# Block 6 wholly in half products, a norm of twelve operations, and other orders at the ends of blocks 1, 2 and 5

## The chip, the cores and the metric

The kernel runs on one core of a Trainium2 chip. The metric is device time in microseconds (us). The engines are named as in the profile: PE is TensorE (matrix products), PEld its weight loads, DVE is VectorE, ACT is ScalarE, POOL is GpSimd, and SP issues transfers.

## What is computed

The reference is a linear attention without softmax, a norm over each head, and a gated GELU layer on its result:

```python
# q, k, v: (8, 8, 576, 64)
kv  = np.einsum('bhsd,bhse->bhde', k, v)
out = np.einsum('bhsd,bhde->bhse', q, kv)
rms = np.sqrt(np.mean(out * out, axis=-1, keepdims=True) + 1e-06)
a   = out / rms * g_norm
x   = a.transpose(0, 2, 1, 3).reshape(4608, 512)     # tokens x channels
# w_gate, w_val: (512, 1536); w_out: (1536, 512); w_res: (512, 512)
g, val   = x @ w_gate, x @ w_val
ffn_out  = (gelu(g) * val) @ w_out
out      = x + sigmoid(x @ w_res) * ffn_out          # (4608, 512)
```

## The kernel before

The 4608 tokens are taken in nine blocks of 512. Blocks 0 to 7 hold 512 of the 576 tokens of batches 0 to 7. Block 8 holds the 64 that are left of each. While block m runs through the gated layer, the attention of batch m+2 is computed beside it, and its result t (FP16) is written as soon as its norm is there.

A block has twelve slices f of the 1536 hidden columns, for the gate (g) and for the value (v). A slice can be done plainly, four products of 128x512 for each of g and v. Or four slices are done as a group in **half products**: seven products of half matrices (256 token columns) in place of eight, after Strassen and Winograd. They need sums of the weights (`ws`), formed once, and sums of the tokens (`ts`), formed once in each block. `GROUPS` says which of the three groups of a block are in half products:

```python
GROUPS = {blk: (1, 2) for blk in range(2, B - 1)} | {B - 1: (1, 0, 2), B: (0, 1, 2)}   # B = 8
```

So blocks 2 to 6 do group 0 plainly, as slices 0 to 3, and blocks 7 and 8 do all three groups in half products. Two helpers compute these pieces:

```python
def m_gval(blk, f, pool=pmoe, tag="mm"):          # one plain slice
    gps = pool.tile([P, NJ * P], FP32, ...);  m_mm(gps, wg_c, f, blk, 0, NJ)   # 4 matmuls 128x512
    vps = pool.tile([P, NJ * P], FP32, ...);  m_mm(vps, wv_c, f, blk, 0, NJ)   # 4 matmuls 128x512
    m_act(blk, f, gps, vps)                       # ACT: ge = gelu(gps);  DVE: hid = ge * vps
# gv_group: a half-product group. A digit is a product (4 matmuls 128x256), E and d are copies
# on ACT, F and c are sums on DVE, g11.. a GELU on ACT, h11.. a product on DVE (h22 on POOL).
for word in """1g 1v Eg 5g Ev 5v dg 6g dv 6v Fg 2g Fv 2v 7g g11 7v cg 3g cv 3v h11 g22 4g
               g12 h12 4v g21 h22 h21""".split():
    ...
    for f in amid.get(word, ()):                  # work of other stages that is placed behind a word
        f()
```

After its groups a block has the products with `w_res` (`rps`) and then the seven half products of the output layer. Between these stand the sums, the gate (`pf`), and the sum with x (`fin`, on POOL). At the places named `aside` other stages put work of theirs:

```python
def others():                                     # second part of a block's output layer
    prod(w["A"], s_[1], wo_t[:, 1], False)
    aside("F");  sub(nc.vector, w["F"], w["A"], w["d"], ALU.add)
    aside("00"); prod(w["E"], ...); pf((0, 0), w["E"])
    aside("22"); prod(w["A"], s_[2], ...)
    c22 = res_all[part((1, 1))]
    sub(nc.vector, c22, w["A"], w["d"], ALU.add)  # reads bank A before it is written again
    aside("01"); prod(w["F"], ...); pf((0, 1), w["F"])
    if not later: fin((0, 0))
    aside("11"); prod(w["A"], ...); pf((1, 1), c22); pf((1, 0), w["A"])
    if later: return                              # block 1: its fins are in block 2
    fin((0, 1)); store(0); fin((1, 1)); fin((1, 0)); store(1)
if later:
    at_word(blk + 1, 0, "h21", *x[0:2], fin((0, 0)), fin((0, 1)), store(0))
    at_word(blk + 1, 1, "Fv", x[2])
    at_word(blk + 1, 1, "h21", x[3], fin((1, 0)), fin((1, 1)), store(1))
# the four sums ts of a block's tokens, on DVE, in the output layer of the block ahead
for blk in GROUPS:
    for key, f in zip(("00", "22", "01", "11"), token_sums(blk, nc.vector)):
        aside_out(blk - 1, key, f)
```

The norm of batch b takes 1/sqrt of a 128x40 tile by an integer guess and three Newton steps. From batch 2 on it runs on POOL with fifteen operations. The scalings `a_t` (t = o times that, on DVE, out of the four PSUM banks of o) follow it:

```python
tensor_scalar(m  = ss / D + eps); tensor_scalar(yy = guess(m)); tensor_scalar(mh = -0.5 * m)
for _ in range(3):
    tensor_tensor(a = yy * yy); tensor_tensor(a = a * mh)
    tensor_scalar(a = a + 1.5); tensor_tensor(yy = a * yy)          # on POOL
...
aside_out(m, "F", lambda: a_norm(b, 0, NJ + rem, pool))             # m = b - 2
at(m, NF + 3, lambda: new_block(b), lambda: a_t(b, 0), lambda: a_t(b, 1))   # behind others()
for j in range(2, NJ + rem):
    at(m + 1, j - 2, lambda j=j: a_t(b, j))                         # behind plain slices 0, 1, 2
```

POOL also issues the loads of q, k and v of the next batch (`load_behind`, behind group 1 of the block). It is in order[...].

Of the kernel before, what the change touches and what calls it, by code (L numbers as in the profile page):

```python
# [8 lines left out]
FP32 = mybir.dt.float32  # L9
# [9 lines left out]
def kernel(  # L19
# [15 lines left out]
    nc = tc.nc  # L35
# [59 lines left out]

    def load_qr(b):
        if b % 2 == 0:
            qr_t[b // 2] = qkvp.tile([P, C], FP16, tag="qr", name="qr")
# [182 lines left out]
        nc.scalar.copy(out=st[b]["kv2"], in_=st[b]["ps"][0])  # L281

    def rem_out(b):
        st[b]["o"][NJ] = o32 = attnp.tile([P, C], FP32, tag="o32", name="o32")
        for e in range(2):
            nc.scalar.copy(
                out=o32.rearrange("p (r e d) -> p r e d", e=2, d=D)[:, :, e, :], in_=st[b]["ps"][1][e]
            )

    def a_norm(b, j0, j1, eng=nc.vector):  # L290

        s = st[b]
        if "rinv" not in s:
            s["rinv"] = attnp.tile([P, NJ + 1, H], FP32, tag="ny", name="ny")
        ss, yy = (t[:, j0:j1, :].rearrange("p j h -> p (j h)") for t in (s["ss"], s["rinv"]))
        n = (j1 - j0) * H
        m = attnp.tile([P, (NJ + 1) * H], FP32, tag="nm", name="nm")[:, 0:n]
        a = attnp.tile([P, (NJ + 1) * H], FP32, tag="na", name="na")[:, 0:n]
        mh = attnp.tile([P, (NJ + 1) * H], FP32, tag="nh", name="nh")[:, 0:n]
        eng.tensor_scalar(out=m, in0=ss, scalar1=1.0 / D, scalar2=RMS_EPS, op0=ALU.mult, op1=ALU.add)  # L300
        eng.tensor_scalar(
            out=yy.bitcast(I32), in0=m.bitcast(I32), scalar1=-0.5, scalar2=float(0x5F3759DF), op0=ALU.mult, op1=ALU.add
        )
        eng.tensor_scalar(out=mh, in0=m, scalar1=-0.5, scalar2=None, op0=ALU.mult)
        for _ in range(3):
            eng.tensor_tensor(out=a, in0=yy, in1=yy, op=ALU.mult)
            eng.tensor_tensor(out=a, in0=a, in1=mh, op=ALU.mult)
            if eng is nc.vector:
                eng.scalar_tensor_tensor(out=yy, in0=a, scalar=1.5, in1=yy, op0=ALU.add, op1=ALU.mult)
            else:  # L310
                eng.tensor_scalar(out=a, in0=a, scalar1=1.5, scalar2=None, op0=ALU.add)
                eng.tensor_tensor(out=yy, in0=a, in1=yy, op=ALU.mult)  # L312

    def pair(b):

# [38 lines left out]
        )  # L354

    def d_rem_qT(b):
        st[b]["qrT"] = attnp.tile([P, NP, P], FP16, tag="qrT", name="qrT")
        nc.sync.dma_start(out=st[b]["qrT"], in_=qr_t[pair(b)], transpose=True)

    def d_xT(b, j0, j1):  # L360
# [127 lines left out]
    def out_by_products(blk, later, banks, amid):  # L488
        w = {}
        s_ = hid_sums  # L490

        def aside(ahead_of):
            for f in amid.get(ahead_of, ()):
                f()

        def res(jj):
            for j in (2 * jj, 2 * jj + 1):
                m_res(blk, j, banks[j])

        def first_two():  # L500
            for n in ("D", "E", "F", "A"):
                w[n] = pmoe.tile([P, 2, CH], FP32, name="w" + n, bank=banks[n])
            w["d"] = finp.tile([P, 2, CH], FP32, tag="wd", bufs=1, name="wd")
            s_last(blk)
            prod(w["A"], a_of(blk, 1, 1), b_of(1, 1), True)
            nc.scalar.copy(out=w["E"], in_=w["A"])
            aside("D")
            prod(w["D"], s_[0], wo_t[:, 0], True)
            nc.scalar.copy(out=w["d"], in_=w["D"])
            aside("gates")  # L510
            for j in range(NJ):
                m_sigmoid(j)

        def part(jj):
            return slice(None), slice(2 * jj[0], 2 * jj[0] + 2), slice(jj[1] * CH, (jj[1] + 1) * CH)

        def pf(jj, src):
            nc.vector.tensor_tensor(out=res_all[part(jj)], in0=th_all[part(jj)], in1=src, op=ALU.mult)  # L518

        def fin(jj):  # L520
            of = part(jj)
            nc.gpsimd.tensor_tensor(out=res_all[of], in0=res_all[of], in1=t_t[blk][of], op=ALU.add)  # L522

        def store(jj):
            dst = out[blk * S : blk * S + M0, :].rearrange("(p j) c -> p j c", j=NJ)
            js = slice(2 * jj, 2 * jj + 2)
            nc.sync.dma_start(out=dst[:, js, :], in_=res_all[:, js, :])

        def others():


            prod(w["A"], s_[1], wo_t[:, 1], False)
            aside("F")
            sub(nc.vector, w["F"], w["A"], w["d"], ALU.add)
# [19 lines left out]
            fin((0, 1))  # L554
            store(0)
            fin((1, 1))
            fin((1, 0))
            store(1)

        if later:  # L560
            x = [lambda j=j: a_x(blk, j) for j in range(NJ)]
            at_word(blk + 1, 0, "h21", *x[0:2], lambda: fin((0, 0)), lambda: fin((0, 1)), lambda: store(0))
            at_word(blk + 1, 1, "Fv", x[2])
            at_word(blk + 1, 1, "h21", x[3], lambda: fin((1, 0)), lambda: fin((1, 1)), lambda: store(1))
        return [lambda: res(0), lambda: res(1), first_two, others]

    def out_last(blk, banks):
# [22 lines left out]
        def run():  # L590
            wa = [bank(1, banks["A"][e]) for e in range(2)]
            wd, we, wf = [bank(2, banks[n]) for n in "DEF"]
            d = finp.tile([P, 2, CH], FP32, tag="wd", bufs=1, name="wd")
# [58 lines left out]
    def weight_sums(unit, eng):  # L652
# [3 lines left out]

        def one(s_, x, y, op):
            if s_ == 0:
                pool, tag = (wpool, f"ws{n}{g}") if g > 0 else (qkvp, "k16")
                gv_sums[unit] = pool.tile([P, 4, 2, 2, P], FP16, tag=tag, name="ws")  # L660
# [189 lines left out]
    for n, t in (("g", moe_w_gate), ("v", moe_w_val)):  # L850
# [4 lines left out]
    ident32 = consts.tile([P, P], FP32, name="ident32")  # L855
    make_identity(nc, ident32)

    zeros = consts.tile([P, C], FP16, name="zeros")
    nc.vector.memset(zeros, 0.0)
    mask = consts.tile([P, P], FP32, name="mask")  # L860
# [15 lines left out]
    grow32 = consts.tile([1, 2, D], FP32, name="grow32")  # L876
    nc.vector.tensor_copy(out=grow32, in_=grow[:, None, :].to_broadcast([1, 2, D]))
    grow16 = consts.tile([1, H, D], FP16, name="grow16")
    nc.vector.tensor_copy(out=grow16, in_=grow[:, None, :].to_broadcast([1, H, D]))
    for t in last_kv[0] + last_kv[1]:  # L880
        nc.vector.memset(t[R:P], 0.0)
# [332 lines left out]
    def banks_of(blk):  # L1214
# [16 lines left out]
                groups[i].update({(u, "A"): a0, (u, "E"): e, (u, "F"): f})  # L1231
        (ga0, ge_, gf, ga1), (va0, ve, vf, va1) = g, v
        if blk not in LAST:
            out_at[blk] = {0: ge_, 1: ga1, 2: ve, 3: ge_, "A": va1, "D": ga1, "E": ve, "F": ge_}
            att_at[blk] = [gf, vf, ga0, va0]
            pmoe.turn = [out_at[blk][n] for n in "DEFA"]
# [128 lines left out]
```

## Time and profile before

| | us |
|---|---|
| time, median of three | 330.12 (329.43 to 330.67) |
| span of the profiled execution | 328.4 |
| PE busy | 317.6 |
| DVE busy | 261.3 |
| ACT busy | 193.3 |
| POOL busy | 143.5 |

Busy time is time with an instruction in work on that engine. The span less PE's busy time is the time in which PE had nothing in work. Where it stood idle, and for whom, is read from the list of waits and from the timelines of single engines.

### The profile page before, as it was taken

To read this page: it belongs to the slowest core of one execution; us is meant where nothing else is said; L and a number is where in the kernel's file an instruction comes from. 1 tells how busy PE (TensorE), PEld (TensorE's weight loads), DVE (VectorE), ACT (ScalarE), POOL (GpSimd) and SP (SyncE) were. 2 spreads that over 40 slices of the span, in tenths; PEclk is the share of its full clock that TensorE was granted. 3 is DMA by queue.
4 is the path that set the end of the run, shared out by engine and by line. 5 is a ranking of instruction groups with operands and counts; after the bars stand their busy time and mean duration, and the time that the engine had idled before them with its cause. 6 is when DMAs were issued, how large, how long until landed. Compare 5 with 4: busy or idle time off the path is not lost.

```text
span 328.4 us, 7217 instructions
## 1 busy us (share of the span) xinstructions
PE 317.6 (97%) x2840; PEld 227.1 (69%) x2840; DVE 261.3 (80%) x474; ACT 193.3 (59%) x351; POOL 143.5 (44%) x222
## 2 busy tenths in 40 slices
PE   8999999999989999899999999999999999999993
PEld 3545655445848785686768686868587888788882
DVE  5777879679598995988887888697889877687754
ACT  3764676465537782668376846674465466636660
POOL 2783333574701498428731974115511331051232
PEclk9999999999999999999999999999999999999998
DMA  8999999898985349577949693800340030011004
GB/s 251 322 204 204 195 204 161 181 189 122 180 85 109 100 98 187 157 140 92 135 147 143 73 153 130 162 1 3 128 82 0 8 123 1 2 64 66 0 3 128
DMA packets 76692, 38.87 MB, mean 118 GB/s; under 512 B 42098, under 2 KB 74354, under 8 KB 76658
## 3 DMA queue, kind: packets, MB, share of 16 engines
q0 software_dynamic: 38752, 17.17, 41.7%
q1 hardware_dynamic: 37328, 20.71, 24.4%
q10 hardware_dynamic: 578, 0.52, 0.5%
q8 instruction: 22, 0.36, 0.5%
q14 instruction: 12, 0.10, 0.1%
HBM read 38.80 MB, written 9.44 MB: 147 GB/s over the span
## 4 chain that ended last, share of the span: by engine, by line
PE 82%; DVE 6%; POOL 5%; DMA 3%; issue 2%; ACT 0%; DVEq 0%; POOLq 0%; ACTq 0%
PE Av L723 9%; PE Ag L723 9%; PE gps L386 9%; PE wA L479 8%; PE vps L386 8%; PE rps L406 7%; PE Fv L723 4%; PE Fg L723 4%; PE fps L423 3%; DMA xT<-t 3%; PE w L479 2%; PE Eg L723 2%; PE Ev L723 2%; PE idle L888 2%; PE wF L479 2%
## 5 line engine op out<-in xcount | busy, mean ns | idle before, releaser
L760 POOL TENSOR_TENSOR hid<-ge,c 128x512 f16<-128x512 f16 x17 | 19.8, 1164 | 88.2 <-ACT ge L754 88.2
L723 PEld LDWEIGHTS <-ws 128*128 128x128 f16 x544 | 53.0, 98 | 7.0 <-issue 0.4
L374 ACT ACTIVATE ge<-gps 128x512 f16<-128x512 f32 x40 | 23.7, 597 | 53.5 <-PE gps L386 53.4
L522 POOL TENSOR_TENSOR osb<-osb,t 128x512 f32<-128x512 f32 x28 | 33.5, 1221 | 25.1 <-DVE osb L518 21.9
L479 PEld LDWEIGHTS <-hid_s 128*128 128x128 f16 x384 | 37.6, 98 | 4.3
L386 PE MATMUL vps<-xT,wv 128*128 128x512 f16 x152 | 39.0, 379 | 1.5 <-DVE hid L375 1.5
L386 PE MATMUL gps<-xT,wg 128*128 128x512 f16 x152 | 39.0, 379 | 0.0
L375 DVE TENSOR_TENSOR hid<-ge,vps 128x512 f16<-128x512 f16 x40 | 27.2, 683 | 9.8 <-PE vps L386 8.8
L406 PE MATMUL rps<-wr,xT 128*128 128x512 f16 x144 | 33.4, 380 | 0.0
L479 PEld LDWEIGHTS <-hid 128*128 128x128 f16 x288 | 28.2, 98 | 6.7 <-issue 1.7
L386 PEld LDWEIGHTS <-wv 128*128 128x128 f16 x152 | 14.9, 98 | 19.6 <-issue 1.8
L386 PEld LDWEIGHTS <-wg 128*128 128x128 f16 x152 | 14.7, 98 | 16.4 <-issue 0.2
L415 ACT ACTIVATE th<-rps 128x512 f32<-128x512 f32 x36 | 21.1, 595 | 8.1 <-PE rps L406 8.1
L744 DVE TENSOR_TENSOR Fg<-Ag,d 128x512 f32<-128x512 f32 x17 | 11.9, 700 | 15.7 <-PE Ag L723 11.6
L254 DVE TENSOR_REDUCE ss<-sq 128x8 f32<-128x512 f32 x32 | 20.1, 677 | 4.7 <-ACT sq L249 4.7
L406 PEld LDWEIGHTS <-xT 128*128 128x128 f16 x144 | 13.5, 98 | 14.2
L723 PEld LDWEIGHTS <-wg 128*128 128x128 f16 x204 | 19.7, 98 | 3.7
L723 PEld LDWEIGHTS <-wv 128*128 128x128 f16 x204 | 20.0, 98 | 2.3
L754 ACT ACTIVATE ge<-c 128x512 f16<-128x512 f32 x17 | 10.7, 630 | 17.1 <-DVE c L744 17.1
L479 PE MATMUL wA<-wo_ts,hid_s 128*128 128x256 f16 x168 | 20.6, 273 | 0.0
L332 DVE TENSOR_TENSOR t<-op,ny 128x512 f16<-128x512 f32 x28 | 18.3, 683 | 2.9 <-POOL ny L312 2.8
L723 PE MATMUL Av<-ts,ws 128*128 128x256 f16 x136 | 20.4, 272 | 0.1
(185 smaller groups left out, 716.7 us busy)
## 6 DMA issues: line engine op xcount, KB each, us to landing
out_dram<-osb SPq DMA_DIRECT2D x14, 512.0 KB, 2.6
qraw<-in_q_dram POOLq DMA_DIRECT2D x7, 512.0 KB, 7.1
k<-in_k_dram POOLq DMA_DIRECT2D x7, 512.0 KB, 9.6
v<-in_v_dram POOLq DMA_DIRECT2D x7, 512.0 KB, 11.7
wg<-in_moe_w_gate_dram POOLq DMA_DIRECT2D x2, 512.0 KB, 8.4
wv<-in_moe_w_val_dram POOLq DMA_DIRECT2D x2, 512.0 KB, 8.9
wo<-in_moe_w_out_dram POOLq DMA_DIRECT2D x2, 512.0 KB, 13.6
out_dram<-osb SPq DMA_DIRECT2D x4, 256.0 KB, 4.4
```

Of the source, the lines that this page charges most:

```text
L254: nc.vector.tensor_reduce(out=out_, in_=sqs.pop((b, i)), op=ALU.add, axis=mybir.AxisListType.X)
L332: nc.vector.tensor_tensor(out=t, in0=o, in1=scale, op=ALU.mult)
L374: nc.scalar.activation(out=ge, in_=gps, func=AF.Gelu)
L375: nc.vector.tensor_tensor(out=hids[blk][:, f, :], in0=ge, in1=vps, op=ALU.mult)
L386: nc.tensor.matmul(ps[:, j0 * P : j1 * P], lhsT=w[:, cc, :], rhs=xT_t[blk][:, j0:j1, cc, :], start=(cc == 0 and j0 == 0), stop=(cc == NP - ...
L406: nc.tensor.matmul(rps, lhsT=xT_t[blk][:, j, cc, :], rhs=wr16[:, cc, :], start=(cc == 0), stop=(cc == NP - 1),)
L415: nc.scalar.activation(out=th, in_=rps, func=AF.Tanh, scale=0.5)
L479: nc.tensor.matmul(ps[:, e - es[0], :], lhsT=a[:, f, e * P : (e + 1) * P], rhs=b[:, f, :], start=(start and e == es[0] and f == 0), stop=( ...
L522: nc.gpsimd.tensor_tensor(out=res_all[of], in0=res_all[of], in1=t_t[blk][of], op=ALU.add)
L723: nc.tensor.matmul(out_[:, r, :], lhsT=lhsT, rhs=rhs, start=(first and r == 0 and c == 0), stop=(c == 1), skip_group_check=True,)
L744: nc.vector.tensor_tensor(out=dst, in0=ps["A", u], in1=sb["d", u], op=ALU.add)
L760: eng.tensor_tensor(out=dst, in0=ge[q], in1=source(q, "v"), op=ALU.mult)
```

## The change

All three groups of block 6 are done in half products. For this the weight sums of group 0 have to be there earlier: they are formed in blocks 2 to 5, in tiles of their own, and no longer in block 6. Space for these tiles comes from single buffers for `qr` and `qrT`, from constants of the start that now lie in the rotating `ge` buffers, and from `wd`, which shares the two `o32` buffers.

Since block 6 begins with a group and has no plain slices, the scalings of batch 7 can't stand behind those. The first two are put ahead of the last gates of block 5 (`"11"`), and the others behind words of block 6. In block 5 the gate that reads bank A comes ahead of the other, and the fourth token sum goes to the end. The norm on POOL has twelve operations in place of fifteen: two steps with other constants, the second of higher order.

In block 1 the four token sums for block 2 go behind all gates. In block 2 the sums of block 1's output with x (`fin`) are placed earlier, behind the word `Fv` of the second group. The fins of all other blocks stand behind the last gate, the second half first.

```diff
-            else: a = a + 1.5;  yy = a * yy        (POOL, three steps)
+        magic = 0x5F1FFFF9 if eng is nc.gpsimd else 0x5F3759DF
+        if eng is nc.gpsimd:
+            for step in range(2):
+                eng.tensor_tensor(out=a, in0=yy, in1=yy, op=ALU.mult)
+                eng.tensor_tensor(out=a, in0=a, in1=m, op=ALU.mult)
+                c = (-0.703952253, 0.703952253 * 2.38924456) if step == 0 else (0.375, -1.25)
+                eng.tensor_scalar(out=mh, in0=a, scalar1=c[0], scalar2=c[1], op0=ALU.mult, op1=ALU.add)
+                if step == 1:
+                    eng.tensor_tensor(out=mh, in0=mh, in1=a, op=ALU.mult)
+                    eng.tensor_scalar(out=mh, in0=mh, scalar1=1.875, scalar2=None, op0=ALU.add)
+                eng.tensor_tensor(out=yy, in0=mh, in1=yy, op=ALU.mult)
+            return
...
-            w["d"] = finp.tile([P, 2, CH], FP32, tag="wd", bufs=1, name="wd")
+            w["d"] = attnp.tile([P, 2, CH], FP32, tag="o32", name="wd")
...
-            if not later:
-                fin((0, 0))
             aside("11")
             prod(w["A"], a_of(blk, 2, 2), wo_t[:, 3], False)
-            pf((1, 1), c22)
-            pf((1, 0), w["A"])
+            if len(GROUPS.get(blk + 1, ())) * GF < NF or blk + 1 >= LAST[0]:
+                pf((1, 1), c22)
+                pf((1, 0), w["A"])
+            else:
+                pf((1, 0), w["A"])
+                pf((1, 1), c22)
+            aside("end")
             if later:
                 return
-            fin((0, 1)); store(0); fin((1, 1)); fin((1, 0)); store(1)
+            for i in (1, 0):
+                fin((i, i)); fin((i, 1 - i)); store(i)
...
-            at_word(blk + 1, 0, "h21", *x[0:2], fin((0, 0)), fin((0, 1)), store(0))
-            at_word(blk + 1, 1, "Fv", x[2])
-            at_word(blk + 1, 1, "h21", x[3], fin((1, 0)), fin((1, 1)), store(1))
+            at_word(blk + 1, 0, "Fv", x[0])
+            at_word(blk + 1, 0, "h21", *x[1:3], fin((0, 0)), fin((0, 1)), store(0))
+            at_word(blk + 1, 1, "Fv", x[3], fin((1, 0)), fin((1, 1)), store(1))
...
-    GROUPS = {blk: (1, 2) for blk in range(2, B - 1)} | {B - 1: (1, 0, 2), B: (0, 1, 2)}
+    GROUPS = {blk: (1, 2) for blk in range(2, B - 2)} | {B - 2: (0, 1, 2), B - 1: (1, 0, 2), B: (0, 1, 2)}
...
-        at(m, NF + 3, lambda: new_block(b), lambda: a_t(b, 0), lambda: a_t(b, 1))
+        first = [lambda: new_block(b), lambda: a_t(b, 0), lambda: a_t(b, 1)]
+        if b == B - 1:
+            aside_out(m, "11", *first)
+        else:
+            at(m, NF + 3, *first)
+        if b == B - 1:                     # behind words of block 6: (group, word, work)
+            (0, "1v", t[2:3]), (0, "Fv", t[3:4]), (0, "h21", t[4:5]),
+            (1, "1v", x[0:2]), (1, "Fv", x[2:3]),
+            (2, "1v", [x[3], d_xT(b, 0, NJ), x[4], d_xT(b, NJ, NJ + 1)])
...
-    for i, f in enumerate(late_sums[0:4]):
-        at_word(B - 2, i // 2, ("Fv", "h21")[i % 2], f)
-    at(B - 2, NF + 1, *late_sums[4:8])
+    for i, f in enumerate(late_sums):
+        at_word(2 + i // 2, i % 2, "Fv", f)
     for blk in GROUPS:
         t = token_sums(blk, nc.vector)
+        if blk == 2:
+            at(blk - 1, NF + 3, *t)
+            continue
+        whole = blk == B - 2 and len(GROUPS[blk]) * GF == NF
-        for key, f in zip(("00", "22", "01", "11"), t):
+        for key, f in zip(("00", "22", "01", "end" if whole else "11"), t):
             aside_out(blk - 1, key, f)
```

More of the change, by code (lines that the diff above doesn't have):

```diff
@@ L97, in load_qr @@
         if b % 2 == 0:
-            qr_t[b // 2] = qkvp.tile([P, C], FP16, tag="qr", name="qr")
+            qr_t[b // 2] = qkvp.tile([P, C], FP16, tag="qr", bufs=1, name="qr")
         half = (b % 2) * R
@@ L283, in rem_out @@
     def rem_out(b):
-        st[b]["o"][NJ] = o32 = attnp.tile([P, C], FP32, tag="o32", name="o32")
+        if b < B - 1:
+            o32 = attnp.tile([P, C], FP32, tag="o32", name="o32")
+        else:
+            o32 = qkvp.tile([P, H, NJ * D], FP16, tag="k16", name="o32")
+            o32 = o32.rearrange("p a b -> p (a b)").bitcast(FP32)[:, 0:C]
+        st[b]["o"][NJ] = o32
         for e in range(2):
@@ L299, in a_norm @@
         mh = attnp.tile([P, (NJ + 1) * H], FP32, tag="nh", name="nh")[:, 0:n]
+        magic = 0x5F1FFFF9 if eng is nc.gpsimd else 0x5F3759DF
         eng.tensor_scalar(out=m, in0=ss, scalar1=1.0 / D, scalar2=RMS_EPS, op0=ALU.mult, op1=ALU.add)
         eng.tensor_scalar(
-            out=yy.bitcast(I32), in0=m.bitcast(I32), scalar1=-0.5, scalar2=float(0x5F3759DF), op0=ALU.mult, op1=ALU.add
+            out=yy.bitcast(I32), in0=m.bitcast(I32), scalar1=-0.5, scalar2=float(magic), op0=ALU.mult, op1=ALU.add
         )
+        if eng is nc.gpsimd:
[9 more added lines that the diff above has]
+            return
         eng.tensor_scalar(out=mh, in0=m, scalar1=-0.5, scalar2=None, op0=ALU.mult)
@@ L307, in a_norm @@
             eng.tensor_tensor(out=a, in0=a, in1=mh, op=ALU.mult)
[L308 to L312, printed above, removed]
+            eng.scalar_tensor_tensor(out=yy, in0=a, scalar=1.5, in1=yy, op0=ALU.add, op1=ALU.mult)
     def pair(b):
@@ L356, in d_rem_qT @@
     def d_rem_qT(b):
-        st[b]["qrT"] = attnp.tile([P, NP, P], FP16, tag="qrT", name="qrT")
+        st[b]["qrT"] = attnp.tile([P, NP, P], FP16, tag="qrT", bufs=1, name="qrT")
         nc.sync.dma_start(out=st[b]["qrT"], in_=qr_t[pair(b)], transpose=True)
@@ L544, in others @@
             pf((0, 1), w["F"])
-            if not later:
-                fin((0, 0))
             aside("11")
             prod(w["A"], a_of(blk, 2, 2), wo_t[:, 3], False)
-            pf((1, 1), c22)
-            pf((1, 0), w["A"])
+            if len(GROUPS.get(blk + 1, ())) * GF < NF or blk + 1 >= LAST[0]:
[5 more added lines that the diff above has]
+            aside("end")
             if later:
                 return
[L554 to L558, printed above, removed]
+            for i in (1, 0):
+                fin((i, i))
+                fin((i, 1 - i))
+                store(i)
         if later:
             x = [lambda j=j: a_x(blk, j) for j in range(NJ)]
-            at_word(blk + 1, 0, "h21", *x[0:2], lambda: fin((0, 0)), lambda: fin((0, 1)), lambda: store(0))
-            at_word(blk + 1, 1, "Fv", x[2])
-            at_word(blk + 1, 1, "h21", x[3], lambda: fin((1, 0)), lambda: fin((1, 1)), lambda: store(1))
+            at_word(blk + 1, 0, "Fv", x[0])
+            at_word(blk + 1, 0, "h21", *x[1:3], lambda: fin((0, 0)), lambda: fin((0, 1)), lambda: store(0))
+            at_word(blk + 1, 1, "Fv", x[3], lambda: fin((1, 0)), lambda: fin((1, 1)), lambda: store(1))
         return [lambda: res(0), lambda: res(1), first_two, others]
@@ L592, in run @@
             wd, we, wf = [bank(2, banks[n]) for n in "DEF"]
-            d = finp.tile([P, 2, CH], FP32, tag="wd", bufs=1, name="wd")
+            d = attnp.tile([P, 2, CH], FP32, tag="o32", name="wd")
             u = attnp.tile([P, 2, CH], FP32, tag="sq", bufs=3, name="u")
@@ L658, in one @@
             if s_ == 0:
-                pool, tag = (wpool, f"ws{n}{g}") if g > 0 else (qkvp, "k16")
-                gv_sums[unit] = pool.tile([P, 4, 2, 2, P], FP16, tag=tag, name="ws")
+                gv_sums[unit] = wpool.tile([P, 4, 2, 2, P], FP16, name=f"ws{n}{g}")
             sums = gv_sums[unit]
@@ L854 @@
         nc.sync.dma_start(out=w_raw[n], in_=t[:, 0 : WCS[0]].rearrange("(cc p) f -> p cc f", p=P))
-    ident32 = consts.tile([P, P], FP32, name="ident32")
+    ident32 = moep.tile([P, P], FP32, tag="ge", name="ident32")
     make_identity(nc, ident32)
-    zeros = consts.tile([P, C], FP16, name="zeros")
+    zeros = moep.tile([P, C], FP16, tag="ge", name="zeros")
     nc.vector.memset(zeros, 0.0)
-    mask = consts.tile([P, P], FP32, name="mask")
+    mask = moep.tile([P, P], FP32, tag="ge", name="mask")
     nc.vector.memset(mask, 0.0)
@@ L875 @@
     )
-    grow32 = consts.tile([1, 2, D], FP32, name="grow32")
+    grow32 = moep.tile([1, 2, D], FP32, tag="ge", name="grow32")
     nc.vector.tensor_copy(out=grow32, in_=grow[:, None, :].to_broadcast([1, 2, D]))
-    grow16 = consts.tile([1, H, D], FP16, name="grow16")
+    grow16 = moep.tile([1, H, D], FP16, tag="ge", name="grow16")
     nc.vector.tensor_copy(out=grow16, in_=grow[:, None, :].to_broadcast([1, H, D]))
@@ L1187, in plan_attn_ahead @@
         aside_out(m, "F", lambda: a_norm(b, 0, NJ + rem, pool))
-        at(m, NF + 3, lambda: new_block(b), lambda: a_t(b, 0), lambda: a_t(b, 1))
+        first = [lambda: new_block(b), lambda: a_t(b, 0), lambda: a_t(b, 1)]
+        if b == B - 1:
+            aside_out(m, "11", *first)
+        else:
+            at(m, NF + 3, *first)
+        if b == B - 1:
+            t = [lambda j=j: a_t(b, j) for j in range(NJ + 1)]
+            x = [lambda j=j: a_x(b, j) for j in range(NJ + 1)]
+            for i, word, fs in (
+                (0, "1v", t[2:3]),
+                (0, "Fv", t[3:4]),
+                (0, "h21", t[4:5]),
+                (1, "1v", x[0:2]),
+                (1, "Fv", x[2:3]),
+                (2, "1v", [x[3], lambda: d_xT(b, 0, NJ), x[4], lambda: d_xT(b, NJ, NJ + 1)]),
+            ):
+                at_word(m + 1, i, word, *fs)
+            return
         for j in range(2, NJ + rem):
@@ L1233, in banks_of @@
         if blk not in LAST:
+            if len(groups) % 2:
+                ga0, ga1, va0, va1, ge_, gf, ve, vf = ga1, ga0, va1, va0, gf, ge_, vf, ve
             out_at[blk] = {0: ge_, 1: ga1, 2: ve, 3: ge_, "A": va1, "D": ga1, "E": ve, "F": ge_}
```

## The prediction

> **What bounds the kernel now.** I read the page's first part first, for which engine is full, and its fourth, for the chain that sets the end.
>
> ```profile
> PE 317.6 (97%) x2840; PEld 227.1 (69%) x2840; DVE 261.3 (80%) x474; ACT 193.3 (59%) x351; POOL 143.5 (44%) x222
> ...
> PE 82%; DVE 6%; POOL 5%; DMA 3%; issue 2%; ACT 0%; DVEq 0%; POOLq 0%; ACTq 0%
> ```
>
> PE is at work in 317.6 of 328.4 us. So time is won in two ways only: less work on PE, or a pause of PE taken away. Of the 10.8 us of pauses some 5.5 are the tail after the last product and 2.3 lie in the first 20 us; the change touches neither. The list of waits names the rest, with the two DVE waits behind them:
>
> ```profile
> PE wA L479 <- DVE osb L454: 1.5, 1, 1.5
> PE vps L386 <- DVE hid L375: 1.5, 1, 1.5
> ...
> DVE t L332 <- POOL ny L312: 2.8, 1, 2.8
> ...
> DVE ts L454 <- DMA xT<-t: 2.4, 1, 2.4
> ```
>
> Each is one wait at one place. The timeline of DVE at the end of block 1 shows the first:
>
> ```profile
> 86.05 0.70 DVE L454 TENSOR_TENSOR wF<-wA,wd 128x512 f32<-128x512 f32 x1 [0.25 <-PE wA L479]
> 89.15 0.51 DVE L454 TENSOR_TENSOR ts<-xT 128x512 f16<-128x512 f16 x1 [2.40 <-DMA xT<-t]
> 89.69 0.69 DVE L518 TENSOR_TENSOR osb<-th,wE 128x512 f32<-128x512 f32 x1
> 90.29 0.42 DVE L454 TENSOR_TENSOR ts<-xT,ts 128x512 f16<-128x512 f16 x1
> 90.63 0.68 DVE L454 TENSOR_TENSOR osb<-wA,wd 128x512 f32<-128x512 f32 x1
> ```
>
> A token sum for block 2 stands ahead of the gate and of c22 (the last line) and waits for the transposed x until 89.15. Bank A is free only when c22 ends at 91.3, and PE's last product waits for it. The second pause is at the start of block 3. Here are the timelines of POOL and then of DVE:
>
> ```profile
> 114.58 3.64 POOL L522 TENSOR_TENSOR osb<-osb,t 128x512 f32<-128x512 f32 x2 [1.85 <-DVE t L346]
> ...
> 118.91 0.98 POOL L120 DMA_DIRECT2D qraw<-in_q_dram  x1 [0.32 <-issue]
> ...
> 124.46 0.49 POOL L300 TENSOR_SCALAR nm<-ss 128x40 f32<-128x40 f32 x1
> ...
> 129.93 0.27 POOL L312 TENSOR_TENSOR ny<-na,ny 128x40 f32<-128x40 f32 x1
> ```
>
> ```profile
> 126.75 0.67 DVE L518 TENSOR_TENSOR osb<-th,wA 128x512 f32<-128x512 f32 x1
> 130.23 1.29 DVE L332 TENSOR_TENSOR t<-op,ny 128x512 f16<-128x512 f32 x2 [2.81 <-POOL ny L312]
> 131.44 0.68 DVE L375 TENSOR_TENSOR hid<-ge,vps 128x512 f16<-128x512 f16 x1
> ```
>
> POOL does block 1's last fins until 118.2, then issues loads until 124.4, and only then starts the norm, whose input DVE finished at 121.0. DVE stands still for it, the `hid` product that frees a PSUM bank comes late, and PE pauses until 132.17.
>
> The third measure is the chain in order of time, at the first product of blocks 5, 6, 7 and 8:
>
> ```profile
> 195.42 0.86 PE gps L386 x4
> ...
> 229.22 0.86 PE gps L386 x4
> ...
> 260.98 0.44 PE Ag L723 x4
> ...
> 291.94 0.44 PE Ag L723 x4
> ```
>
> Block 5 takes 33.80 us, block 6 31.76 and block 7 30.96. Blocks 6 and 7 both run without a pause of PE and neither has attention beside it: they differ in that block 7 has its third group in half products too.
>
> [...] four of 256 take 0.44 us and four of 512 take 0.86. [...] So half products lose nothing by being short. [...] the fifteen operations on 40 elements take 5.75 us, 0.38 each, at 124.46 to 130.2. [...] the same kind of operation (`na` at L311) took 0.31 to 0.64 us, and at 223.93 to 230.2 the fifteen took 6.25, 0.42 each.
>
> **The change part by part.**
>
> (1) Block 1's token sums go behind the gates. Product s_2 ends at about 88.6, c22 follows at once (0.7 us) and is done while PE does the next product (1.31 us). Then PE doesn't wait: 1.49 us won. The sums themselves are needed only after block 2's plain slices, 6.9 us later. DVE then has three gates, four sums (0.35 each) and two scalings (0.6 each) ahead of the first `hid`; I get its end at 95.3 and PE's need of its bank at 95.5. That is tight, but holds.
>
> (2) In block 2 the last fins go from behind h21 to behind Fv of the second group. Four fins take 4.6 us; POOL was idle for 14.3 us before the first h22 and partly between the two. In times of the trace before, less 1.5: fins until about 110.7, h22 until 111.9, loads issued from 112.5 to 118.0, norm from 119.5 (when its input is there) to 124.1 (12 x 0.38). DVE reaches the scalings at 125.9, so there is no wait. Block 3 took 126.37 to 161.88 = 35.51; block 4 33.54. The difference, 1.97 us, is all won. It contains the pause of 1.48 and some small ones that follow it.
>
> (3) The norm of twelve: 3 x 0.38 = 1.1 us less for each of six batches, all beside PE. By itself it would be worth something in block 3 only, where (2) has already removed the wait, and in block 5, where (5) needs it.
>
> (4) Block 6: 8 x 0.866 = 6.93 us of plain products become 14 x 0.437 = 6.11: 0.81 us won. The chain says the same, 31.76 - 30.96 = 0.80. DVE gets 7 operations for 4 there, but loses the weight sums (8 x 0.48 us), which go to blocks 2 to 5 with 0.48 us in each group. Before, block 6 carried one behind Fv as well (at 239.62) and PE didn't wait.
>
> (5) The start of block 6. Norm 7 began at 223.93; with twelve at 0.42 it ends at 228.9. DVE reaches the two early scalings at 228.6, so they run from 228.9 to 230.1, then the gate of bank A until 230.7, the other until 231.3, a sum until 231.7, scaling three until 232.3, then Fg and Fv until 233.5. PE would start at 229.22 and ask for these at: 5g 230.1 (scaling one, done), 5v 230.5 (scaling two, done), 6v 231.4 (copy Ev, which needs the gate of A: 231.4 to 231.5), 7g 232.85 (Fg read, 232.95), 7v 233.45 (Fv read, 233.6). After that DVE catches up. I add up 0.1 + 0.15 + 0.2 and, for another link of this kind, set a loss of 0.5 us.
>
> Sum: 1.49 + 1.97 + 0.81 - 0.5 = 3.77 us. 330.12 - 3.8 = **326.3 us**, 1.1% less.
>
> **The rivals.** First, DVE becomes the bound of block 6 (worse than in 5): in group 0, 6.1 us long, I count 1.55 us of leftovers and ten operations at 0.61, 7.65 us. If PE follows this fully, 1.5 us is lost rather than 0.5, and (4) is a loss: 327.3. Against it speaks that half of these operations are behind what PE needs. Second, the shared buffers: `wd` in `o32` waits for h22 on POOL, one `qrT` for the products with it, the constants for `ge`. I looked at who is last in each: h22 ends at 112.7, the copy to `wd` is at 120.05; so I expect nothing. If one holds, each block from 2 to 5 loses some tenths: 327 to 328. Third, the pause of block 1 is only moved: `hid` on DVE comes too late for the third slice of block 2, and 0.5 to 1 us comes back: 327. [...]
>
> **Range and chances.** With nothing lost I get 330.12 - 4.27 = 325.85; runs of the kernel before spread by 0.6 to either side of the median. So the low end is 325.2. The high end takes two rivals at once: 328.2. Faster by over 2% needs under 323.5, more than all pauses concerned and the saved products give: 0.02. Slower by over 2% needs a new stall of some 10 us: 0.02. Within 2%: 0.96.
>
> **What would show it.** Right: the two waits of PE above are gone; wA has no wait on `osb`; DVE's wait on `ny` in block 3 is gone, and the loads there are issued some 6 us earlier; block 3 takes 33.5 us; block 6 takes 31.0 to 31.5, with PE waits on DVE at its start of 0.5 us in all; the twelve operations take 4.6 to 5.0 us. Wrong: PE waits in blocks 2 to 5 that weren't there, on `d`, `wd` or `hid`; a wait of DVE on `ny` ahead of block 5's last gates of more than 0.5 us; block 6 longer than 31.76.

## The result, and the profile after

| | before | changed |
|---|---|---|
| time, median (range), us | 329.77 (329.38 to 330.67) | 326.25 (326.03 to 326.76) |
| span of the profiled execution, us | 328.4 | 324.2 |
| PE busy, us | 317.6 | 316.1 |

The median before is here one of four runs (329.77), where the table ahead of the prediction has three of them (330.12). The ratio is 0.9892, with a 95% interval of 0.9866 to 0.9917: 3.5 us less. The page of the changed kernel, its first part and the chain that sets the end:

```profile
PE 316.1 (97%) x2864; PEld 229.2 (71%) x2864; DVE 260.2 (80%) x477; ACT 194.6 (60%) x355; POOL 135.4 (42%) x205
...
PE 93%; DVE 2%; DMA 2%; SPq 1%; POOL 0%; issue 0%; DVEq 0%
```

DVE's share of the chain falls from 6% to 2% and POOL's from 5% to 0%. The list of what PE waited for keeps only waits of the first 20 us (those of block 6, further down, are too short for it). Its two longest:

```profile
PE idle L901 <- DVE zeros L872: 1.2, 1, 1.2
PE vps L1025 <- DVE t L999: 0.3, 1, 0.3
```

The timeline of DVE at the end of block 1 no longer has a transfer in it. Here c22 (second line) runs as soon as its product is there, and the first token sum (last line) comes behind all gates:

```profile
87.24 0.69 DVE L531 TENSOR_TENSOR osb<-th,wE 128x512 f32<-128x512 f32 x1 [0.60 <-PE wE L492]
88.49 0.69 DVE L467 TENSOR_TENSOR osb<-wA,wd 128x512 f32<-128x512 f32 x1 [0.57 <-PE wA L492]
...
91.72 0.42 DVE L467 TENSOR_TENSOR ts<-xT 128x512 f16<-128x512 f16 x1
```

The timeline of POOL in block 2: the last two fins stand ahead of h22, so loads are issued from 113.73 (118.91 before), and the norm ends at 123.98 instead of 130.20. Of these differences 1.76 us are block 2's earlier start:

```profile
108.93 2.27 POOL L535 TENSOR_TENSOR osb<-osb,t 128x512 f32<-128x512 f32 x2 [0.77 <-DVE t L359]
111.16 1.16 POOL L773 TENSOR_TENSOR hid<-ge,c 128x512 f16<-128x512 f16 x1
...
113.73 0.97 POOL L120 DMA_DIRECT2D qraw<-in_q_dram  x1 [0.32 <-issue]
...
119.52 0.22 POOL L306 TENSOR_SCALAR nm<-ss 128x40 f32<-128x40 f32 x1 [0.32 <-DVE ss L254]
...
123.71 0.27 POOL L319 TENSOR_TENSOR ny<-nh,ny 128x40 f32<-128x40 f32 x1
```

DVE's first scalings at 125.53 show no wait in front of them:

```profile
124.94 0.68 DVE L531 TENSOR_TENSOR osb<-th,wA 128x512 f32<-128x512 f32 x1
125.53 1.28 DVE L345 TENSOR_TENSOR t<-op,ny 128x512 f16<-128x512 f32 x2
```

The chain of the changed kernel at the first product of blocks 5 to 8; block 6 now begins with a group:

```profile
191.75 0.86 PE gps L399 x4
...
225.56 0.44 PE Ag L736 x4
...
256.85 0.44 PE Ag L736 x4
...
287.82 0.44 PE Ag L736 x4
```

The table below is made in the same way for every kernel, from the times at which PE starts the first product of a block. The first column is the start of block 2, in which a pause of block 1 shows; the next six are the lengths of blocks 2 to 7. All are in us.

| kernel | start of 2 | 2 | 3 | 4 | 5 | 6 | 7 | median, us |
|---|---|---|---|---|---|---|---|---|
| before | 92.67 | 33.54 | 35.51 | 33.54 | 33.80 | 31.75 | 30.97 | 329.77 |
| changed | 90.91 | 33.59 | 33.54 | 33.55 | 33.80 | 31.30 | 30.96 | 326.25 |
| token sums amid the gates | 93.96 | 34.55 | 33.55 | 33.54 | 33.80 | 31.30 | 31.02 | 328.09 |
| two fins late | 90.94 | 33.59 | 33.63 | 33.54 | 33.80 | 31.30 | 30.96 | 326.18 |
| norm of fifteen | 90.97 | 33.59 | 33.54 | 33.54 | 33.81 | 32.37 | 30.96 | 327.48 |
| x and fins as before | 91.82 | 33.54 | 34.64 | 33.54 | 33.80 | 31.31 | 30.97 | 327.36 |
| these and the norm of fifteen | 91.18 | 33.54 | 35.83 | 33.54 | 33.81 | 32.38 | 30.96 | 329.65 |
| group 0 of block 6 plain | 90.93 | 33.60 | 33.54 | 33.54 | 33.80 | 31.76 | 30.96 | 326.88 |
| scalings behind the gates | 91.61 | 33.60 | 33.54 | 33.54 | 33.80 | 32.80 | 30.97 | 327.85 |
| scalings three, four later | 91.30 | 33.59 | 33.55 | 33.54 | 33.80 | 31.52 | 30.96 | 326.85 |
| all for batch 7 later | 90.96 | 33.59 | 33.54 | 33.55 | 33.80 | 32.26 | 30.96 | 327.45 |
| three extra operations | 91.17 | 33.59 | 33.55 | 35.21 | 33.80 | 31.28 | 31.03 | 328.07 |
| five extra operations | 92.00 | 33.59 | 33.54 | 37.78 | 34.35 | 31.30 | 31.21 | 331.79 |
| changed, once more | 91.89 | 33.59 | 33.54 | 33.54 | 33.81 | 31.30 | 30.96 | 326.64 |

Block lengths repeat within 0.1 us where nothing was changed, with one exception (31.21). The start of block 2 varies by up to 1.1 us with the opening. So I read an effect from the block's length, and take the median as a second witness. It is a weaker one: the rows come from four comparisons, partly on different chips, in which the kernel before had medians from 329.77 to 330.44.

### The profile page after: what moved, and what is told of

It reads as the page before. It is cut to its first block, busy times and chain, and to the rows that moved or that the text cites. A ratio compares the mean times of both kernels' runs of the same rounds, so it can differ in the third digit from the quotient of the medians.

```text
span 324.2 us, 7256 instructions
## 1 busy us (share of the span) xinstructions
PE 316.1 (97%) x2864; PEld 229.2 (71%) x2864; DVE 260.2 (80%) x477; ACT 194.6 (60%) x355; POOL 135.4 (42%) x205
## 4 chain that ended last, share of the span: by engine, by line
PE 93%; DVE 2%; DMA 2%; SPq 1%; POOL 0%; issue 0%; DVEq 0%
PE wA L492 11%; PE Av L736 10%; PE Ag L736 10%; PE rps L419 10%; PE gps L399 9%; PE vps L399 9%; PE Fv L736 5%; PE Fg L736 5%; PE fps L436 3%; PE wF L492 3%; PE wE L492 3%; PE wD L492 3%; PE w L492 2%; PE Eg L736 2%; PE Ev L736 2%; PE kvp L208 2%
## 5 line engine op out<-in xcount | busy, mean ns | idle before, releaser
L773 POOL TENSOR_TENSOR hid<-ge,c 128x512 f16<-128x512 f16 x18 | 20.9, 1163 | 83.9 <-ACT ge L767 83.9
L387 ACT ACTIVATE ge<-gps 128x512 f16<-128x512 f32 x36 | 21.3, 597 | 42.3 <-PE gps L399 42.2
L535 POOL TENSOR_TENSOR osb<-osb,t 128x512 f32<-128x512 f32 x28 | 31.7, 1162 | 32.8 <-DVE osb L531 31.0
L399 PE MATMUL gps<-xT,wg 128*128 128x512 f16 x136 | 34.9, 379 | 0.0
L399 PE MATMUL vps<-xT,wv 128*128 128x512 f16 x136 | 34.9, 379 | 0.0
L388 DVE TENSOR_TENSOR hid<-ge,vps 128x512 f16<-128x512 f16 x36 | 24.4, 683 | 9.2 <-PE vps L399 8.6
L736 PEld LDWEIGHTS <-wsv 128*128 128x128 f16 x288 | 28.1, 98 | 3.9 <-issue 0.3
L736 PEld LDWEIGHTS <-wsg 128*128 128x128 f16 x288 | 28.1, 98 | 3.4
L736 PE MATMUL Av<-ts,wsv 128*128 128x256 f16 x144 | 21.6, 272 | 0.0
L736 PE MATMUL Ag<-ts,wsg 128*128 128x256 f16 x144 | 21.6, 273 | 0.0
```

The lines of the kernel that those rows point to most:

```text
L387: nc.scalar.activation(out=ge, in_=gps, func=AF.Gelu)
L388: nc.vector.tensor_tensor(out=hids[blk][:, f, :], in0=ge, in1=vps, op=ALU.mult)
L399: nc.tensor.matmul(ps[:, j0 * P : j1 * P], lhsT=w[:, cc, :], rhs=xT_t[blk][:, j0:j1, cc, :], start=(cc == 0 and j0 == 0), stop=(cc == NP - ...
L736: nc.tensor.matmul(out_[:, r, :], lhsT=lhsT, rhs=rhs, start=(first and r == 0 and c == 0), stop=(c == 1), skip_group_check=True,)
L773: eng.tensor_tensor(out=dst, in0=ge[q], in1=source(q, "v"), op=ALU.mult)
```

## The experiments

### The token sums of block 1

```diff
-        if blk == 2:
-            at(blk - 1, NF + 3, *t)
-            continue
```

> The changed kernel with the four token sums for block 2 put back between the gates of block 1; all else stays. Theory (c22 stood behind a token sum that waits for the transposed x): the pause of PE ahead of block 1's last product is back, block 2 starts 1.65 us later than in the changed kernel (1.5 of it as a wait of wA on DVE), every later block has its old length, and the time is about 1.6 us above the changed kernel's. Rival (the transfer itself, or the later pause, set the time; the gain came from block 3): block 2 starts at most 0.3 us later.

Measured: ratio to the kernel before 0.9943 (0.9921 to 0.9965), 1.8 us above the changed kernel. The rival falls: the pause is back, on the transfer and on nothing else. DVE waited 3.05 us for x, with c22 behind the sum.

```profile
89.71 0.42 DVE L467 TENSOR_TENSOR ts<-xT 128x512 f16<-128x512 f16 x1 [3.05 <-DMA xT<-t]
```

But this execution lost 3.05 us at the start of block 2, and another 0.96 in block 2. The timeline of PE and its granted clock in windows of 1 us (the column ahead of the last two) show why:

```profile
91.94 2.23 PE L492 MATMUL wA<-wo_ts,hid 128*128 128x256 f16 x12 [2.16 <-DVE osb L467]
93.96 1.92 PE L399 MATMUL gps<-xT,wg 128*128 128x512 f16 x4
```

```profile
92.00:93.00 1.00, 1.00 (x8) 0.81 (x8) 1.00 (x3) 0.00 (x0) 0.00 (x0) 0.74 2.02 166
93.00:94.00 1.00, 1.00 (x7) 0.69 (x6) 0.75 (x2) 0.00 (x0) 0.00 (x0) 0.50 1.89 144
...
95.00:96.00 1.00, 1.00 (x4) 0.30 (x2) 1.00 (x2) 0.09 (x1) 0.00 (x0) 0.55 0.36 23
```

Behind the pause of 2.16 us the clock was at half for about 3.4 us (0.52 + 1 + 1 + 0.9), and twelve products took 2.23 us instead of 1.47. So the expectation of 1.65 us was too simple: the order is the cause, but its cost depends on when x lands, and a stretch at half clock can come on top. The times agree: this kernel's runs lie between 326.17 (the changed kernel's level) and 330.09, the changed kernel's between 326.03 and 326.76. That the quickest ones are executions in which x landed early is argued; no trace shows one. The profiled execution is the slowest of the twenty. In eleven of the others the mean granted clock was 0.996 or more, while 3.4 us at half clock alone would lower it to 0.995: in those no such stretch followed.

### Does the clock follow from the pause alone?

An operation on DVE that nobody needs, `scr = th * wA`, three or five times ahead of c22 in block 4 (shortened here):

```diff
+            if blk == 4:
+                scr = attnp.tile([P, 2, CH], FP32, tag="sq", bufs=3, name="scr")
+                for _ in range(3):          # or 5
+                    sub(nc.vector, scr, th_all[:, 0, :], w["A"], ALU.mult)
             c22 = res_all[part((1, 1))]
             sub(nc.vector, c22, w["A"], w["d"], ALU.add)
```

> The changed kernel with three extra operations on DVE in block 4 (a product of the gate and bank A into a tile that nobody reads), ahead of c22, so that PE's last product there waits. They make a pause of PE with no transfer involved. Theory (a pause costs its own length up to about 2 us, and above that PE's clock falls to half for some 3 us more, as it did after the 2.16 us of the run with the token sums amid the gates): a pause of about 1.1 us, block 4 is 1.2 us longer, the clock stays full. Rival (any pause lowers the clock): 2 us longer or more.

> As the run with three extra operations on DVE, with five. Theory: a pause of about 2.3 us, the clock falls to half for some 3 us behind it, and block 4 with the start of block 5 is 4 us longer in all. Rival (the fall of the clock in that other run had to do with the transfers beside it): 2.4 us longer at full clock.

The 2 us in the first theory was my estimate from the 2.16 us of the run above. Three operations made a pause of 1.51 us (I had expected 1.1); the clock stayed at 1.00 and block 4 grew by 1.67 us. That is the pause and 0.16, the tail of the last product that still counts as busy. PE's last product and the clock:

```profile
192.21 1.47 PE L492 MATMUL wA<-wo_ts,hid 128*128 128x256 f16 x12 [1.51 <-DVE osb L467]
```

```profile
193.00:194.00 1.00, 1.00 (x10) 0.71 (x8) 1.00 (x4) 0.00 (x0) 0.00 (x0) 1.00 0.00 0
```

Five made one of 2.95 us. The same views of that kernel:

```profile
194.48 2.64 PE L492 MATMUL wA<-wo_ts,hid 128*128 128x256 f16 x12 [2.95 <-DVE osb L467]
```

```profile
194.00:195.00 1.00, 0.52 (x4) 0.37 (x4) 1.00 (x3) 0.00 (x0) 0.00 (x0) 0.80 0.00 0
195.00:196.00 1.00, 1.00 (x6) 0.73 (x5) 1.00 (x3) 0.00 (x0) 0.00 (x0) 0.50 0.00 0
```

Blocks 4 and 5 together grew by 4.8 us: 3.1 of pause and 1.7 of half clock. PE waits for DVE here, and no transfer ran when the clock fell (the last two numbers of these lines are 0). Transfers had run beside the first part of the pause (120 GB/s at 192 to 193 us), but also with three operations (124 GB/s at 191 to 192 us), where the clock stayed at 1.00. So the rival falls as far as these two traces go. The median tells the same, 5.2 us above that of the changed kernel beside it (326.64). But the half clock doesn't follow each time: in three of the sixteen runs (329.47 to 330.10 us) the mean granted clock was 0.995 or 0.996, in the other thirteen (331.12 to 333.43 us) 0.990 to 0.993. One stretch of 3.4 us at half clock would lower the mean by 0.005 (an estimate from the span of 330 us), which is about the difference. The operations that make the pause are the same in all sixteen, so its length alone doesn't seem to decide.

### Fins and norm in block 2

Undone were, one after the other, the place of the last two fins; the norm; the place of x and all fins; and the last two together.

```diff
# two fins late
-            at_word(blk + 1, 1, "Fv", x[3], fin((1, 0)), fin((1, 1)), store(1))
+            at_word(blk + 1, 1, "Fv", x[3])
+            at_word(blk + 1, 1, "h21", fin((1, 0)), fin((1, 1)), store(1))
```

> The changed kernel with the last two fins of block 1 and their store put back behind h21 of block 2's second group; the norm keeps its twelve operations. Theory (the place of the fins and the length of the norm share block 3's pause): loads are issued some 4 us later, the norm starts at about 122.8 and ends at 127.4, DVE waits 1.9 us for it, and block 3 is 0.6 us longer than in the changed kernel (33.5), not 2.0. Rival one (the place of the fins alone did it): block 3 is 1.9 to 2.0 longer. Rival two (the short norm alone did it): no difference.

Block 3 grew by 0.09 us only. Rival two seemed right, but the trace says why it isn't: x[3] had stayed at its early place, so the fins followed h22 at 111.40 without waiting, and the norm ended at 126.6. DVE waited 0.97 us for it and PE lost next to nothing:

```profile
126.67 1.29 DVE L345 TENSOR_TENSOR t<-op,ny 128x512 f16<-128x512 f32 x2 [0.97 <-POOL ny L319]
```

So DVE has about 1 us of slack here, which I had not seen.

```diff
# norm of fifteen (in short): the twelve operations out, the three steps back
-            for step in range(2): ...          # 5 + 5 operations
+            mh = -0.5 * m; for _ in range(3): a = yy*yy; a = a*mh; a = a+1.5; yy = a*yy
```

> The changed kernel with the norm of fifteen operations. Theory (the short norm is worth nothing where the norm lies beside other work, but in block 5 it now stands ahead of the first scalings and the gate of bank A): blocks 2 to 5 keep their lengths, DVE waits 1.6 us for the norm of batch 7, and block 6 is 1.6 us longer (32.9 against 31.3). Rival one (the operations count wherever they are): each of blocks 2 to 5 is 0.3 us longer or more. Rival two (DVE has slack there): block 6 within 0.3 us of 31.3.

Blocks 2 to 5 kept their lengths: with the fins early the short norm is worth nothing there. Block 6 grew by 1.07 us. DVE's wait in this kernel:

```profile
226.03 1.29 DVE L338 TENSOR_TENSOR t<-op,ny 128x512 f16<-128x512 f32 x2 [1.00 <-POOL ny L318]
```

A wait of 1.00 us became 1.07 us of time, one to one. I had expected 1.6, because I took 0.42 us for an operation; the fifteen took 5.7 us here, 0.38 each.

```diff
# x and fins as before (and, in the fourth, the norm of fifteen too)
-            at_word(blk + 1, 0, "Fv", x[0])
-            at_word(blk + 1, 0, "h21", *x[1:3], fin((0, 0)), fin((0, 1)), store(0))
-            at_word(blk + 1, 1, "Fv", x[3], fin((1, 0)), fin((1, 1)), store(1))
+            at_word(blk + 1, 0, "h21", *x[0:2], fin((0, 0)), fin((0, 1)), store(0))
+            at_word(blk + 1, 1, "Fv", x[2])
+            at_word(blk + 1, 1, "h21", x[3], fin((1, 0)), fin((1, 1)), store(1))
```

> The changed kernel with all of block 2's work for block 1 (the products x and the fins) at the words where the kernel before has it; the norm keeps twelve operations. The run with only the fins put back lengthened block 3 by 0.09 us: there the last x stayed early, so its fins came 1.5 us before those of the kernel before, and DVE waited 0.97 us for the norm without PE noticing. Theory (DVE has about 1 us of slack at block 3's start, and the norm's length and the place of x and fins draw on it together): DVE waits 1.5 to 1.9 us for the norm and block 3 takes 33.9 to 34.2 us against 33.54. Rival (the short norm alone removed the pause): 33.6 or less.

> As the run with x and fins as before, and the norm of fifteen operations as well. Theory (the pause needs both): DVE waits 2.8 us for the norm, block 3 takes 35.3 to 35.5 us as in the kernel before, and block 6 1.07 us longer (32.37, as with the norm of fifteen alone). Rival (what is new in blocks 1 and 2, sums and buffers, has a part in it): block 3 below 34.5.

With the short norm, DVE waited 2.0 us for it, PE waited 0.6, and block 3 took 34.64. With the long one it waited 3.2 us, and PE:

```profile
PE vps L392 <- DVE hid L381: 1.8, 1, 1.8
```

Block 3 took 35.83, more than the kernel before's 35.51. Read as a square, block 3 costs:

| | norm of twelve | norm of fifteen |
|---|---|---|
| x and fins early | 33.54 | 33.54 |
| x and fins as before | 34.64 | 35.83 |

The place of x and fins, moved together, is sufficient on its own; the norm on its own takes off 1.19 us and leaves 1.10. Both of my numbers were low: I had forecast up to 34.2, and 35.3 to 35.5. In the fourth kernel the norm starts 1.35 us ahead of block 3 and in the kernel before 1.75. The first difference ahead of it is at the word Fv of block 2's second group, where x[2] now stands behind a weight sum that the kernel before doesn't have there. In the trace of the third kernel, where the order is the same, the sum took 0.89 us (at 108.50) beside the fins on POOL, and what follows in the group is 0.4 us later than before. That this weight sum alone makes the 0.3 us wasn't tried.

### Block 6

```diff
-    GROUPS = {... range(2, B - 2)} | {B - 2: (0, 1, 2), B - 1: ...}
+    GROUPS = {... range(2, B - 1)} | {B - 1: ...}          # and the scalings of batch 7 as for other batches
```

> The changed kernel with group 0 of block 6 done plainly again, and so with the scalings of batch 7 and the gates of block 5 where they were; the weight sums stay in blocks 2 to 5. Theory (half products win 0.81 us of PE and lose 0.33 us at the start of the block): block 6 takes 31.76 us against 31.29, blocks 2 to 5 as in the changed kernel, the time about 0.5 us above. Rival (the weight sums were what block 6 paid for, or DVE bounds it): block 6 is as long as in the changed kernel or shorter.

As expected: 31.76 us, 0.46 more, with the weight sums still in blocks 2 to 5. The rival falls.

```diff
-            aside_out(m, "11", *first)          # for batch 7
+            at(m, NF + 3, *first)
```

> The changed kernel with the first two scalings of batch 7 behind the last gates of block 5, where the other batches have them; block 6 stays in half products and the norm has twelve operations. Theory (product 5g of block 6 waits for the bank that scaling one frees, and DVE reaches it only after two gates and a sum): PE waits 1.5 to 1.7 us in group 0, block 6 takes 32.7 us against 31.3 in the changed kernel, other blocks unchanged. Rival (these waits run beside others that the gates ahead of them shorten): block 6 within 0.3 us of 31.3.

Block 6 took 32.80, 1.50 more. Product 5g waited for the bank of o that the first scaling frees:

```profile
PE Fg L736 <- DVE t L345: 1.5, 1, 1.5
```

So half products in block 6 without the early scalings are a loss of 1.05 us against the kernel before (31.75).

Then I tried to take away what was left at the start of block 6. This is DVE in the changed kernel, and under it PE. DVE does two scalings, two gates, a token sum and a third scaling ahead of Fg:

```profile
224.90 1.29 DVE L345 TENSOR_TENSOR t<-op,ny 128x512 f16<-128x512 f32 x2
226.11 0.68 DVE L531 TENSOR_TENSOR osb<-th,wA 128x512 f32<-128x512 f32 x1
226.70 0.68 DVE L531 TENSOR_TENSOR osb<-th,osb 128x512 f32<-128x512 f32 x1
227.31 0.42 DVE L467 TENSOR_TENSOR ts<-xT,ts 128x512 f16<-128x512 f16 x1
227.64 0.68 DVE L345 TENSOR_TENSOR t<-op,ny 128x512 f16<-128x512 f32 x1
228.24 0.69 DVE L757 TENSOR_TENSOR Fg<-Ag,d 128x512 f32<-128x512 f32 x1
```

```profile
228.45 0.60 PE L736 MATMUL Ev<-xT,wv 128*128 128x256 f16 x4
228.98 0.60 PE L736 MATMUL Ag<-ts,wsg 128*128 128x256 f16 x4
229.58 0.60 PE L736 MATMUL Av<-ts,wsv 128*128 128x256 f16 x4
```

Without a wait four products start 0.44 us after the last four; here it is 0.53 and 0.60, because 7g and 7v need Fg and Fv to have read bank A.

```diff
-                (0, "1v", t[2:3]),
-                (0, "Fv", t[3:4]),
+                (0, "Fv", t[2:3]),
+                (0, "cv", t[3:4]),
```

> The changed kernel with scaling three of batch 7 behind the word Fv of block 6's group 0 (not 1v), and scaling four behind cv (not Fv). Theory (what is left of the pause at block 6's start, 0.33 us, is DVE doing a scaling ahead of Fg and Fv that group 0 doesn't need yet): block 6 takes 31.0 us against 31.3, the time is 0.3 us less. Rival (the 0.33 us come from the gate of bank A and the copy Ev behind it): 31.3 as in the changed kernel.

Both theories missed: 31.52. The waits of group 0 went (0.06 us left), but Fg of group 1 came late instead, and PE lost 0.5 us there, at 7g and 7v (the last two lines):

```profile
235.00 0.60 PE L736 MATMUL Ev<-xT,wv 128*128 128x256 f16 x4
235.78 0.60 PE L736 MATMUL Ag<-ts,wsg 128*128 128x256 f16 x4 [0.18 <-DVE Fg L757]
236.38 0.60 PE L736 MATMUL Av<-ts,wsv 128*128 128x256 f16 x4
```

The waits weren't due to one scaling, but to a DVE that is at work almost without a break from 224.9 to 239 in both kernels.

```diff
# on top of the last
-                (0, "h21", t[4:5]), (1, "1v", x[0:2]), (1, "Fv", x[2:3]), (2, "1v", [x[3], ...]),
+                (1, "Fv", t[4:5]), (1, "cv", x[0:2]), (1, "h21", x[2:4]), (2, "1v", [...]),
```

> The changed kernel with all that block 6 does for batch 7 behind words at which DVE has time: scaling three behind Fv and four behind cv of group 0, scaling five behind Fv of group 1, the products x behind cv and h21 of group 1. The run that only put scalings three and four later took the waits out of group 0 (0.06 us left) and got 0.5 us of them in group 1, where Fg came late. Theory (DVE has a backlog that is worked off over two groups, and only what PE doesn't ask for may stand in it): no waits in either group, block 6 31.0 us against 31.3, the time 0.3 us less than the changed kernel's. Rival (the backlog itself is the bound): 31.3 to 31.5, with the waits in group 1 or 2.

> The changed kernel once more, unchanged, on the same chip as the run that puts all work for batch 7 later: block 6 31.3 us, 326.3 us.

The theory held for groups 0 and 1, which have no more wait than 0.05 us. Yet block 6 took 32.26, and the time was 0.8 us above that of the changed kernel beside it. The timelines of DVE, POOL and PE at the end of group 1:

```profile
237.10 1.74 DVE L359 TENSOR_TENSOR t<-t,g 128x512 f16<-128x512 f16 x2
```

```profile
237.39 1.17 POOL L773 TENSOR_TENSOR hid<-ge,c 128x512 f16<-128x512 f16 x1 [4.13 <-ACT ge L767]
```

```profile
239.49 0.61 PE L736 MATMUL Fv<-ts,wsv 128*128 128x256 f16 x4 [0.30 <-DVE hid L773]
```

Two products x, which took 0.75 us elsewhere (0.75 at 239.09 in the changed kernel), took 1.74 beside h22 on POOL, h11 and h12 behind them came 1 us late, and group 2 paid for it. I know of no better order from these runs; x at a word where POOL is idle wasn't tried. The changed kernel stays the best one here.

## Why the prediction was right

**Time.** 326.3 forecast, 326.25 measured. That they agree so closely is luck in part: the sum of steps was 3.77 us, the two profiled executions differ by 4.1, the medians by 3.5. Of the 4.1 us 0.11 come from the opening, which the change doesn't mean to touch. One thing the prediction didn't see: what the token sums ahead of c22 cost, which it took for a fixed 1.49 us, is not the same in each execution. Over the comparisons with the runs below, the kernel before took 328.50 to 332.80 us (three runs over 1.5% above its fastest are left out), the changed kernel 326.03 to 327.05 in its eight. The spread comes back with one edit, the token sums amid the gates: 326.17 to 330.09 in twenty runs, where twenty runs of "these and the norm of fifteen", with the sums behind the gates, span 1.5 us. In the six slowest of those runs of the kernel before, from 332.40 on, the mean granted clock was 0.991 or 0.992, in the others at least 0.995. That these six had a longer pause with half clock behind it fits, but no trace shows one of them.

**(1) Token sums.** Right in mechanism, low in size. Forecast 1.49, lost in the profiled execution 1.65: the wait as listed leaves out 0.16 us in which the tail of the last product still counts as busy. Such a wait has to be read from start to start. DVE's first `hid` of block 2 ended at 95.06 (forecast 95.3) and PE took up its bank at 95.23.

**(2) Fins.** Right: 35.51 became 33.54. The square shows that this step alone gives all of it, as the prediction had it, and that the norm gives nothing on top. The forecast path came true: norm from 119.52 to 123.98 (119.5 to 124.1 forecast), DVE at the scalings at 125.53 (125.9). Loads came 5.2 us earlier, where some 6 were forecast. What it overlooked is why the old place was so slow: two fins took 3.64 us there and 2.27 at the new one. At the old place they ran beside this sum on DVE, which took 0.96 us at 114.63 in the changed kernel, with no fin beside it:

```profile
115.41 1.80 DVE L454 TENSOR_TENSOR hid_s<-hid_s,hid 128x1536 f16<-128x1536 f16 x1
```

So 1.37 us of what the new place saves on POOL go with what the fins run beside.

**(3) Norm.** Right: 4.5 us for twelve in block 2 and 4.6 in block 5, where fifteen cost 1.07 us of PE's time. My 0.42 per operation for block 5 was too much; it was 0.38 in both forms.

**(4) Half products.** Right: 0.81 less the next item would be 0.48, and block 6 went from 31.75 to 31.30, and back to 31.76 when it was undone.

**(5) Start of block 6.** Right in mechanism, 0.2 us too high: forecast 0.5, measured 0.33, which is 31.30 less the 30.96 of block 7. The norm ended at 224.9, just as DVE came to it, so the chain of DVE ran 0.3 us earlier against PE than I had worked out; 6v had no wait, 7g and 7v had 0.09 and 0.16, and two later products 0.04 each.

**Rivals.** DVE as bound of block 6 is half true: it never rests over two groups, and PE pays 0.33 us for it, not 1.5. Shared buffers cost nothing that shows: blocks 4 and 5 have their old lengths. The pause of block 1 wasn't moved: block 2 has no pause of PE. Fins beside group work cost nothing that shows: block 2 is 0.05 us longer with the fins early or late, and has its old length where x is as before.

## What to carry to other kernels

Put nothing that waits for a transfer ahead of what frees a buffer of the bounding engine. DVE took c22 only behind a token sum that waited 2.40 us for x in the profile before and 3.05 us in the run with the sums amid the gates; PE lost 1.65 us in the one and 3.05 in the other, so one profile doesn't give the cost. If two changes work on the same pause, undoing them one at a time in the finished kernel can show too little for each (here nothing for the norm and 1.10 of 2.29 us for the place of x and fins): make the square of all four. Work that moves to "where the engine has time" has to be looked at for whom it then runs beside, too: two products x took 1.74 us beside h22 and 0.75 where no operation of POOL ran.

## What the runs showed of the hardware

PE's clock. After pauses of 1.49 us (the kernel before, block 1), 1.48 (the kernel before, block 3), 1.51 (three extra operations) and 1.80 us (x and fins as before with the norm of fifteen) the granted clock stayed at 1.00. Behind those of 2.16 us (the token sums amid the gates) and 2.95 us (five extra operations) it was at 0.50 for 3.4 us. These runs give no length from which on it falls: with five operations the mean granted clock was 0.990 to 0.993 in thirteen of sixteen runs and 0.995 or 0.996 in the other three. Counted from the end of PE's last product ahead of the pause, the clock fell after 2.7 us with the token sums amid the gates and after 3.1 us with five operations. Behind the last product of the whole kernel it fell after 3.4 us in the profile before and after 2.4 us in that of the changed kernel. What decides between the two isn't shown.

DVE and POOL. Some operations on DVE took longer beside one on POOL: two products x took 1.74 us beside h22 of 1.17 us in the kernel with all for batch 7 later, and 0.75 in the changed kernel at 239.09, with no operation of POOL beside them. A sum of `hid_s` took 1.80 us beside the fins of the kernel before, and 0.96 in the changed kernel at 114.63, with no fin beside it. The fins took 1.8 us each there, and 1.14 in the changed kernel at 108.93. Three DVE operations that read one input from a PSUM bank took 0.67 to 0.69 us beside those fins (at 109.37, 109.97 and 110.69). What makes the ones slower and not the others isn't shown.
